# Turning the normed x by transposing DMAs instead of by TensorE, in a new order of steps

## Chip, cores and metric

The kernel runs on one core of a Trainium2 chip. The metric is the device time of one execution in microseconds, as the median of several runs. The profile is of one further execution of the same program.

## What is computed

The inputs are bfloat16. S is 2048 tokens, D is 640 channels, F is 1728.

```python
x  = A_q                                   # (1, 2048, 640)
xn = layernorm(x)                          # (x - mean) / sqrt(var + 1e-5)
# branch A: a long convolution over the tokens, gated by xn
k_shift = causal 4-tap filter of A_k along the tokens, taps A_shift_k per channel
kv = k_shift * A_v
y  = irfft(rfft(kv, padded to 2S) * rfft(A_ssm_k, padded to 2S))[:S] + kv * A_ssm_D
A  = xn * y
# branch B: a gated feed-forward layer
g, u = xn @ B_w_gate, xn @ B_w_up          # (2048, 1728) each
B  = (sigmoid(g) * u) @ B_w_down
out = x + A + B
```

## The kernel before

**Layout.** Token 16p + b lies on partition p in block b, so x and xn are 128 x 16 x 640 tiles. Four blocks of 128 tokens make a group (512 tokens); the feed-forward branch works through groups 0 to 3 as tiles t = 0 to 3. The convolution branch works through five chunks c of 128 channels, each over all tokens.

**Feed-forward branch, per tile.** TensorE needs xn with the channels on the partitions: the tile xnT, 128 x (4 blocks) x (5 channel chunks) x 128, of which there is one buffer for all groups. `xn_mm` transposes a block by five TensorE transposes into a PSUM tile pt, and `xn_ev` copies pt to xnT on ScalarE. For each of 13 slices of 128 columns of F there are a gate product (`gate_mm`, 5 matmuls of 128x128 by 128x512), an up product (`up_mm`), the sigmoid on ScalarE (`gate_ev`) and the product of the two into hT on VectorE (`up_ev`); the last 64 gate and up columns share one product (`both_mm`). Then come 16 halves of down products (`down_mm`, 7 matmuls of 128x320 each), and VectorE adds each finished one to x (`down_ev`). All four blocks of xnT must be there before the first gate product of a tile, and the last reader of xnT in a tile is its `both_mm`. Group 0 is normed and turned ahead of everything, block by block, with small quarter products between; the statistics and norm of groups 1 to 3 are VectorE steps (`ln_norms`, `ln_var`, `ln_xn`) with one small GpSimd step between (`ln_pow`).

**Convolution branch, per chunk.** The transform is a two-stage matrix product. VectorE filters k in two halves of 8 steps (`kv_op`) and turns the filter A_ssm_k (`h_turn`). Stage one (`st1_mm`, 8 matmuls a step, 8 steps a chunk) is evicted (`st1_ev`, 128x1024), written to DRAM (`wr1`) and read back in another layout (`rd2`, tile t). Stage two (`st2_mm`, 16 matmuls of 32x32) is evicted in two halves (`st2_ev`, tile xz), multiplied by VectorE in a shuffle and a product (`prod`), transformed back (`inv1_mm`, 32 matmuls of 32x32), evicted in two halves (`inv1_ev`, tiles ao and kx), written to DRAM (`wr2`) and read back (`rdb`, tiles bi and kx). The last stage (`inv2_mm`, tile psb) is multiplied with xn (`inv2_q`) and added to x (`inv2_x`) on VectorE. Finished parts of x are stored (`store`).

**Queues and order.** Every engine runs its instructions in the order in which the program issues them. After the start (group 0, the first weights, 14.6 us in the profile), that order is written out by hand: each kind of step is a chain under one letter, and a string ORDER says from which chain the next step is taken. Nearly all DMAs are issued by SyncE (SP), in this same order, so a DMA whose wait is not over holds back every DMA behind it. The letters that matter here: g products of the feed-forward branch, s and u their ScalarE and VectorE steps, k the filter of k, l the norm, e and E the turning of a group, a/A, b/B, c/C, d/q the stages of the convolution with their evictions, w, r, W, R its DRAM traffic, m and n the loads, o the stores. A letter F, J, I or Y stands for B, C, A or E with the eviction on VectorE instead of ScalarE; the old string has none of them.

**PSUM.** Two pools: psC (2 buffers of 128x1024 float32) for the stages of the convolution and for pt of group 0; psG (4 buffers of one 512-column bank) for gate, up and down products, psb, and pt of groups 1 to 3.

Of the kernel before, what the change touches and what calls it, by code (L numbers as in the profile page):

```python
# [10 lines left out]
BF16 = mybir.dt.bfloat16  # L11
# [8 lines left out]
P = 128  # L20
NB = S // P
NC = DM // P
# [35 lines left out]
def kernel(  # L58
# [14 lines left out]
    nc = tc.nc  # L73
# [11 lines left out]
    TBd = nc.inline_tensor(tbbits, name="tabTB")  # L85
    SMd = nc.inline_tensor(smbits, name="tabSM")
# [4 lines left out]
    psC = ctx.enter_context(tc.tile_pool(name="psC", bufs=2, space=bass.MemoryType.PSUM))  # L91
    psG = ctx.enter_context(tc.tile_pool(name="psG", bufs=4, space=bass.MemoryType.PSUM))

    ident = res.tile([P, P], BF16, name="ident")
# [4 lines left out]
    TBt = res.tile([P, 2, NB, P], U16, name="TBt")  # L99
    SMt = res.tile([P, 3, 32], U16, name="SMt")  # L100
# [5 lines left out]
    xn = res.tile([P, NB, DM], BF16, name="xn")  # L106
    xnT = res.tile([P, 4, NC, P], BF16, name="xnT")
# [13 lines left out]
    sync = nc.sync  # L121
# [105 lines left out]

    xts = {}

    def xn_mm(g, i):  # L230
        pool, tag = (psG, "g") if g else (psC, "c")
        xts[i] = pt = pool.tile([P, NC, P], BF16, name="pt", tag=tag)
        for c in range(NC):
            nc.tensor.transpose(pt[:, c, :], xn[:, 4 * g + i, c * P:(c + 1) * P], ident[:])  # L234

    def xn_ev(g, i, copy=act_copy):
        copy(out=xnT[:, i, :, :], in_=xts[i][:, :, :])


    sig = {}  # L240
# [246 lines left out]
            nc.tensor.matmul(idle[:, :], lhsT=hT[:, 0, 0:P], rhs=hT[:, 0, :], start=True, stop=True)  # L487

    def turn(i):
        xn_mm(0, i)  # L490
        xn_ev(0, i)


    busy(15)
    for i in range(4):
# [5 lines left out]
        ln_pow(0, i, i + 1)  # L501
    ln_xn(0, 3)
    turn(0)
    busy(2)
    for i in range(4):
        for fc in range(2):
            for u in range(2):
                quarter(u, fc, i)
            if (i, fc) in ((0, 0), (1, 0), (1, 1)):
                turn(1 + i + fc)  # L510
# [2 lines left out]
        up_ev(0, fc)  # L513


    chains = {k: [] for k in "ABCDEHKPRTVWZabcdeghklmnopqrstuw"}

    def step(k, fn, *args):
        chains[k].append((fn, args))
# [16 lines left out]
    def hs(c):  # L536
        return [(load_h, c)]

    def ks(c):
        return [(load_halo, c), (load_k, c, 0, 8), (load_k, c, 8, NB)]  # L540

    def vs(c):
        return [(load_v, c, 0, 8), (load_v, c, 8, NB)]

    for k in ((load_w, sync, 512, 768, 0),
              (load_w, sync, 512, 768, 1),
              (load_taps, 0),
              (sync.dma_start, SMt[:], SMd.ap()),
              (load_w, sync, 768, 1024, 0),
              (load_w, sync, 768, 1024, 1),  # L550
              (load_w, sync, 1024, 1280, 0),
              (load_w, sync, 1024, 1280, 1),
              (load_wd, sync, 0, 7),
              *ks(0),
              (load_w, sync, 1280, FF, 0),
              (load_w, sync, 1280, FF, 1),
              *hs(0),
              *vs(0),
              (load_wd, sync, 7, NFC),
              (sync.dma_start, S1t[:], S1d.ap()),  # L560
              *hs(1),
              (load_x, sync, 1),
              *ks(1),
              *vs(1)):
        step("m", *k)
    for k in ((load_x, sync, 2), (load_x, sync, 3), (sync.dma_start, TBt[:], TBd.ap())):
        step("n", *k)
    step("Z", taps, 0)

# [38 lines left out]
    for g in range(1, 4):  # L608
        for i in range(4):
            step("l", ln_norms, g, i)  # L610
        step("l", ln_var, g, 0, 4)
        step("P", ln_pow, g, 0, 4)
        for i in range(4):
            step("l", ln_xn, g, i)
        for i in range(4):
            step("e", xn_mm, g, i)
            step("E", xn_ev, g, i)

    for b in range(0, 12, 2):
        step("o", store, b, b + 2, 0, 4 * P)  # L620
# [5 lines left out]
    step("o", store, NB - 1, NB, 4 * P, DM)  # L626

    ORDER = """
    mmmmmmmmmmZgmgsmgumgsmgugsgugsmgugskgkugkskgumkgsmkgumkgsmTguHgsHDgumgskkgukgskmgukgskgumkgkmgmutmkm
    auTaAHgAHDagAwlhauaAlglaglguwlgkPkgAulgAllleKeuKwEekaEekaEgkEVVHAgAHDgwughkgkugkskguKrrkaskaAgkAkguw  # L630
    gkskgutkgTskgkKuKaksaAKkgAkaugAwkaksaAkgkwakAgVuAVHasgwHDAauhgAkgkskwbugBrkgBkktbgpBrTkgBpsapsaAuguA
    apKgKswAkaugAkaKkwsakgVHAVgAuDHgswkcugCkgkskCgnuWakaAkgAkgukwbguBrlgBlgulbgBrlgBuglkPpgnulgllleenuEe
    kbEeprgEEgptkBgupBgkaauAgpAkapgswAkaugAkawksaAgkAkguwlcsglCgClbusgrlBWgBkugslpPkaauAgllAlglspwbgBruR
    kgBkscpguCpgCksWbkgBrugBkksbpgBrudBpdgsRqpcqgCqugCqpsWbgBrukgBspbgBrupdBadqsaApRgqAqapgwAqauseeEueaE
    egEEgAgAwaudAdqgwqRqcugCqgCguWbgBrgBugpbpdBrdqgBuqgqpcqgCupgCguWbgBrgBugpspRbgBrugBspcguCpgsCguWbsdr
    BdqgRBqqguqbpsgrBpgBugpspcgCugCsWbguBrdBgqspbqgBupgBspgucpsdCgRqRCqguWbsgBgBugpspgudsdqcqgCqoqdCudqg
    WqqgsqgugoguRRguggugguogodudqogqqogqdoudqogqqogqguogooouo
    """
    left = {k: iter(v) for k, v in chains.items()}
    for k in "".join(ORDER.split()):  # L640
# [33 lines left out]
```

## Time and profile before

| | |
|---|---|
| Runs, median of 3 (lowest to highest) | 239.77 us (239.52 to 239.82) |
| The profiled execution's own time | 240.16 us |
| Its span, first to last instruction | 238.4 us |
| Granted TensorE clock | 1.000 |
| Busy: TensorE (matmul) / VectorE / ScalarE / GpSimd | 232.6 / 190.5 / 140.9 / 11.2 us |
| DMA: bytes, mean rate | 54.82 MB, 230 GB/s |
| DMA: share of the 16 engines, main queue | 81.3% |

The profile gives for each engine its busy time and, in 40 slices of 5.96 us, its busy share in tenths; then the chain of work that ended last, the groups of instructions by line, tile and shape with their mean duration, and the DMAs with their median time from issue to landing. A duration in it is that of one instruction from start to end; matmuls overlap in a pipeline, so what a matmul costs in a row of its kind is read from the chain. A DMA share above 1 in a window means that packets overlap on the engines.

### The profile page before, as it was taken

How to read it: one execution, taken by the hardware profiler on the slowest of the kernel's cores; microseconds unless marked ns; L12 is line 12 of the kernel's file. 1: busy time of each engine (PE TensorE's matmuls, PEld its weight loads, DVE VectorE, ACT ScalarE, POOL GpSimd, SP SyncE). 2: the span in 40 equal slices, each digit the busy share in tenths (PEclk: the TensorE clock that was granted, in tenths of full speed). 3: DMA queues.
4: the chain of work that ended last, by engine and by line, in shares of the span. 5: the costliest groups of instructions: out<-in, count | busy, mean ns of one | idle time of the engine just before them, and what ended most of it. 6: DMA issues, size and time to landing. Idle time of an engine off the chain costs nothing.

```text
span 238.4 us, 5555 instructions
## 1 busy us (share of the span) xinstructions
PE 232.6 (98%) x2265; PEld 134.8 (57%) x2265; DVE 190.5 (80%) x350; ACT 140.9 (59%) x178; POOL 11.2 (5%) x24
## 2 busy tenths in 40 slices
PE   8899999999999999999999999999999999999994
PEld 2664445877555555667754434577664434456772
DVE  4633989999999999999999999865585695968372
ACT  2343322728557898764888787997558858764000
POOL 5210000020000000002000000000000000000000
PEclk9999999999999999999999999999999999999999
DMA  7999999998998999998444889875849795285494
GB/s 213 291 315 236 254 326 294 197 257 236 251 312 252 259 292 292 297 252 313 154 179 143 235 237 265 216 231 202 230 119 223 186 282 126 83 241 145 123 303 137
DMA packets 89119, 54.82 MB, mean 230 GB/s; under 512 B 47814, under 2 KB 83206, under 8 KB 88838
## 3 DMA queue, kind: packets, MB, share of 16 engines
q1 hardware_dynamic: 88150, 53.66, 81.3%
q10 hardware_dynamic: 944, 0.82, 1.1%
q8 instruction: 17, 0.28, 0.5%
q14 instruction: 8, 0.07, 0.1%
HBM read 36.12 MB, written 18.35 MB: 228 GB/s over the span
## 4 chain that ended last, share of the span: by engine, by line
PE 91%; DMA 5%; ACT 2%; issue 0%; ACTq 0%; DVE 0%
PE pd L301 26%; PE pg L257 22%; PE pu L257 22%; PE psb L461 4%; PE ps L360 3%; PE ps L362 3%; PE ps L393 3%; DMA w<-in_B_w_up_dram 3%; PE psa L422 2%; PE pg L278 2%; PE pt L234 2%; DMA d<-t 2%; ACT t L223 1%; PE pu L248 1%; PE pg L248 1%
## 5 line engine op out<-in xcount | busy, mean ns | idle before, releaser
L257 PEld LDWEIGHTS <-w 128*128 128x128 bf16 x500 | 46.4, 98 | 54.4 <-issue 5.3
L301 PE MATMUL pd<-wd,hT 128*128 128x320 bf16 (+2 forms) x448 | 64.3, 299 | 0.0
L257 PE MATMUL pg<-xnT,w 128*128 128x512 bf16 x250 | 62.2, 379 | 0.0
L257 PE MATMUL pu<-xnT,w 128*128 128x512 bf16 x250 | 62.2, 379 | 0.0
L301 PEld LDWEIGHTS <-hT 128*128 128x128 bf16 x448 | 42.3, 98 | 18.5 <-issue 1.7
L266 ACT ACTIVATE sig<-pg 128x512 bf16<-128x512 f32 x52 | 31.3, 605 | 29.8 <-PE pg L257 28.0
L272 DVE TENSOR_TENSOR hT<-sig,pu 128x512 bf16<-128x512 bf16 x52 | 35.2, 680 | 15.5 <-PE pu L257 9.6
L223 ACT CAST t<-ps 128x1024 bf16<-128x1024 f32 x40 | 39.2, 1023 | 12.1 <-DMA d<-t 7.9
L223 ACT CAST xz<-ps 128x1024 bf16<-128x1024 f32 x40 | 38.5, 1017 | 10.6 <-PE ps L393 10.5
L306 DVE TENSOR_TENSOR x<-pd,x 128x320 bf16<-128x320 f32 (+2 forms) x32 | 15.3, 479 | 15.5 <-PE pd L301 15.3
L408 DVE TENSOR_TENSOR xz<-xz 128x2048 bf16<-128x2048 bf16 x20 | 24.3, 1217 | 0.2
L360 PE MATMUL ps<-kvh,S1t 128*128 128x128 bf16 x160 | 21.2, 217 | 0.5 <-ACT t L223 0.5
L362 PE MATMUL ps<-kvh,S1t 128*128 128x128 bf16 x160 | 21.2, 220 | 0.0
L340 DVE TENSOR_TENSOR acc<-acc,tmp 128x1024 bf16<-128x1024 bf16 x30 | 20.7, 689 | 0.6
L338 DVE TENSOR_TENSOR tmp<-kx,sc 128x1024 bf16<-128x1024 bf16 x30 | 20.5, 685 | 0.4
L223 ACT CAST ao<-psa 128x1024 bf16<-128x1024 f32 x16 | 15.6, 1014 | 6.0 <-PE psa L422 3.9
L362 PEld LDWEIGHTS <-S1t 128*128 128x128 bf16 x160 | 15.4, 96 | 2.9 <-issue 0.8
L466 DVE TENSOR_TENSOR yx<-psb,xn 128x512 bf16<-128x512 f32 x20 | 13.8, 690 | 3.9 <-PE psb L461 2.9
L360 PEld LDWEIGHTS <-S1t 128*128 128x128 bf16 x160 | 15.5, 97 | 2.3
L223 ACT COPY xnT<-pt 128x640 bf16<-128x640 bf16 x16 | 10.2, 708 | 10.9 <-PE pt L234 10.6
L198 DVE BATCH_NORM_STATS2 st<-x 128x6 f32<-128x320 bf16 x32 | 13.7, 470 | 2.6 <-DMA x<-in_A_q_dram 2.6
L406 DVE STREAM_SHUFFLE xz<-xz 128x512 f32<-128x512 f32 x20 | 14.5, 725 | 0.0
(44 smaller groups left out, 147.5 us busy)
## 6 DMA issues: line engine op xcount, KB each, us to landing
d<-t SPq DMA_DIRECT2D x20, 512.0 KB, 3.9
t<-d SPq DMA_DIRECT2D x20, 512.0 KB, 5.2
bi<-d SPq DMA_DIRECT2D x8, 512.0 KB, 5.2
d<-ao SPq DMA_DIRECT2D x6, 512.0 KB, 4.1
kx<-in_A_k_dram SPq DMA_DIRECT2D x10, 256.0 KB, 5.1
hn<-in_A_ssm_k_dram SPq DMA_DIRECT2D x20, 128.0 KB, 5.9
kvh<-in_A_v_dram SPq DMA_DIRECT2D x10, 256.0 KB, 5.3
x<-in_A_q_dram SPq DMA_DIRECT2D x3, 640.0 KB
```

Source lines behind the costliest of these rows:

```text
L223: nc.scalar.copy(out=out, in_=in_)
L257: nc.tensor.matmul(pg[:, :], lhsT=w[:, c, u * UP + fc * P:u * UP + (fc + 1) * P], rhs=xnT[:, :, c, :], start=(c == 0), stop=(c == NC - 1))
L266: nc.scalar.activation(sig[fc][:, :], pgs[0, fc][:, :], ACT.Sigmoid)
L272: nc.vector.tensor_tensor(hT[:, fc, :], sig[fc][:, :], pgs[1, fc][:, :], ALU.mult)
L301: nc.tensor.matmul(pd[:, :], lhsT=hT[:, fc, bb * P:(bb + 1) * P], rhs=wd[:, fc, es], start=(fc == 0), stop=(fc == NFC - 1))
L306: nc.vector.tensor_tensor(x[:, 4 * t + bb, es], pds[bb, half][:, :], x[:, 4 * t + bb, es], ALU.add)
L338: nc.vector.tensor_tensor(d["tmp"][:, :, :], kx[:, lo + 3 - m:hi + 3 - m, :], sb(m), ALU.mult)
L340: nc.vector.tensor_tensor(d["acc"][:, :, :], d["acc"][:, :, :], d["tmp"][:, :, :], ALU.add)
L360: nc.tensor.matmul(ps[:, i, 0:P], lhsT=S1[:, b, h, :], rhs=cin[c]["kvh"][:, 0, b, :], start=True, stop=True)
L362: nc.tensor.matmul(ps[:, i, P:2 * P], lhsT=S1[:, b, h, :], rhs=hp[:, b // 2, b % 2, :], start=True, stop=True)
L406: nc.vector.stream_shuffle(z[:, 2, :, :].bitcast(F32), z[:, 1, :, :].bitcast(F32), swap)
L408: nc.vector.tensor_tensor(z[:, 1:3, :, :], z[:, 0:1, :, :].to_broadcast((P, 2, 8, P)), z[:, 1:3, :, :], ALU.mult)
```

## The change

Group 0 is still turned by TensorE. For groups 1 to 3 the five transposes and the copy of each block are replaced by one transposing DMA from SP, `xn_turn`, which reads 128 x 640 of xn and writes 128 x 5 x 128 of xnT. There are 12 of them. The chain E goes, and so do the pt tiles in psG. The order of the first loads is new (x of group 1 stands first), the chain n begins with the table TBt and not with x of group 2, and the whole ORDER string is new. It also moves six evictions to VectorE (F twice, I once, J three times).

```diff
--- before.py
+++ after.py
@@ -227,14 +227,17 @@
 
     xts = {}
 
-    def xn_mm(g, i):
-        pool, tag = (psG, "g") if g else (psC, "c")
-        xts[i] = pt = pool.tile([P, NC, P], BF16, name="pt", tag=tag)
+    def xn_mm(i):
+        xts[i] = pt = psC.tile([P, NC, P], BF16, name="pt", tag="c")
         for c in range(NC):
-            nc.tensor.transpose(pt[:, c, :], xn[:, 4 * g + i, c * P:(c + 1) * P], ident[:])
-
-    def xn_ev(g, i, copy=act_copy):
-        copy(out=xnT[:, i, :, :], in_=xts[i][:, :, :])
+            nc.tensor.transpose(pt[:, c, :], xn[:, i, c * P:(c + 1) * P], ident[:])
+
+    def xn_ev(i):
+        nc.scalar.copy(out=xnT[:, i, :, :], in_=xts[i][:, :, :])
+
+
+    def xn_turn(g, i):
+        sync.dma_start_transpose(xnT[:, i, :, :], xn[:, 4 * g + i, :])
 
 
     sig = {}
@@ -487,8 +490,8 @@
             nc.tensor.matmul(idle[:, :], lhsT=hT[:, 0, 0:P], rhs=hT[:, 0, :], start=True, stop=True)
 
     def turn(i):
-        xn_mm(0, i)
-        xn_ev(0, i)
+        xn_mm(i)
+        xn_ev(i)
 
 
     busy(15)
@@ -513,7 +516,7 @@
         up_ev(0, fc)
 
 
-    chains = {k: [] for k in "ABCDEHKPRTVWZabcdeghklmnopqrstuw"}
+    chains = {k: [] for k in "ABCDHKPRTVWZabcdeghklmnopqrstuw"}
 
     def step(k, fn, *args):
         chains[k].append((fn, args))
@@ -542,28 +545,28 @@
     def vs(c):
         return [(load_v, c, 0, 8), (load_v, c, 8, NB)]
 
-    for k in ((load_w, sync, 512, 768, 0),
+    for k in ((load_x, sync, 1),
+              (load_w, sync, 512, 768, 0),
               (load_w, sync, 512, 768, 1),
-              (load_taps, 0),
-              (sync.dma_start, SMt[:], SMd.ap()),
               (load_w, sync, 768, 1024, 0),
               (load_w, sync, 768, 1024, 1),
+              (load_taps, 0),
+              *vs(0),
               (load_w, sync, 1024, 1280, 0),
               (load_w, sync, 1024, 1280, 1),
-              (load_wd, sync, 0, 7),
-              *ks(0),
               (load_w, sync, 1280, FF, 0),
               (load_w, sync, 1280, FF, 1),
               *hs(0),
-              *vs(0),
+              (load_wd, sync, 0, 7),
               (load_wd, sync, 7, NFC),
+              *ks(0),
+              *ks(1),
+              *hs(1),
               (sync.dma_start, S1t[:], S1d.ap()),
-              *hs(1),
-              (load_x, sync, 1),
-              *ks(1),
+              (sync.dma_start, SMt[:], SMd.ap()),
               *vs(1)):
         step("m", *k)
-    for k in ((load_x, sync, 2), (load_x, sync, 3), (sync.dma_start, TBt[:], TBd.ap())):
+    for k in ((sync.dma_start, TBt[:], TBd.ap()), (load_x, sync, 2), (load_x, sync, 3)):
         step("n", *k)
     step("Z", taps, 0)
 
@@ -613,8 +616,7 @@
         for i in range(4):
             step("l", ln_xn, g, i)
         for i in range(4):
-            step("e", xn_mm, g, i)
-            step("E", xn_ev, g, i)
+            step("e", xn_turn, g, i)
 
     for b in range(0, 12, 2):
         step("o", store, b, b + 2, 0, 4 * P)
@@ -626,15 +628,15 @@
     step("o", store, NB - 1, NB, 4 * P, DM)
 
     ORDER = """
-    mmmmmmmmmmZgmgsmgumgsmgugsgugsmgugskgkugkskgumkgsmkgumkgsmTguHgsHDgumgskkgukgskmgukgskgumkgkmgmutmkm
-    auTaAHgAHDagAwlhauaAlglaglguwlgkPkgAulgAllleKeuKwEekaEekaEgkEVVHAgAHDgwughkgkugkskguKrrkaskaAgkAkguw
-    gkskgutkgTskgkKuKaksaAKkgAkaugAwkaksaAkgkwakAgVuAVHasgwHDAauhgAkgkskwbugBrkgBkktbgpBrTkgBpsapsaAuguA
-    apKgKswAkaugAkaKkwsakgVHAVgAuDHgswkcugCkgkskCgnuWakaAkgAkgukwbguBrlgBlgulbgBrlgBuglkPpgnulgllleenuEe
-    kbEeprgEEgptkBgupBgkaauAgpAkapgswAkaugAkawksaAgkAkguwlcsglCgClbusgrlBWgBkugslpPkaauAgllAlglspwbgBruR
-    kgBkscpguCpgCksWbkgBrugBkksbpgBrudBpdgsRqpcqgCqugCqpsWbgBrukgBspbgBrupdBadqsaApRgqAqapgwAqauseeEueaE
-    egEEgAgAwaudAdqgwqRqcugCqgCguWbgBrgBugpbpdBrdqgBuqgqpcqgCupgCguWbgBrgBugpspRbgBrugBspcguCpgsCguWbsdr
-    BdqgRBqqguqbpsgrBpgBugpspcgCugCsWbguBrdBgqspbqgBupgBspgucpsdCgRqRCqguWbsgBgBugpspgudsdqcqgCqoqdCudqg
-    WqqgsqgugoguRRguggugguogodudqogqqogqdoudqogqqogqguogooouo
+    mmmmmmmmmmgmgsgZuTgmsgumgsgugsgumgsgumgsgllugHsmmguDmHgsmlguglsmgulPgsmmgulglsllgkmugksmmegukgmkeguH
+    geuDgHegukhgkgukgkgknuakaAkgkAgukwgkgunKkgKktKgTukaskaAgkAkaugAwklansaAglwlagVuVAgHsHgADugwshlgulgkP
+    skgulrglsrllgukgskkaauAgkAkgskwgukbskgrBKkgBuKKtapsaTkgApAaugAwkaksaAgkkwaugAVHVAgHDswbugBrkhgBkksbg
+    uBrpgBkepsaaAgueApgkwcpegCuekgCugkWkbugBrkglKBgKlKbugpBrlgBugpgupclgCpgCugWlkPbtugkBTlrglBllsapRaAug
+    pAagkswAkauaAkgkwaskgVAHVdAudDgqRwHcsqgCqkgCqubWskgBkrgBkuapsaAkddpAgqwbugBrqqgBkqsbpgBrupgBskgpcusp
+    gCgCkuWbksgrBFgupbsgkBRpgButcpsgkCpgCuaWskaAgkAkdudwaqRaAkgqAqaekgsqAuawgekAkgwkebugkBekdBduaqrapArg
+    qAqgpwgquckgCJguWkbgkBrkgBukgpRbugpBrgBkgupapaAgAaudAwdqaRaqAqgqwasgAIguwcsgCJduWdqbgBrqqgBqspbguBrp
+    gBspgugpsbugBrFgspcugpCgCsWbguBrgBspbguBRpRgBspgucpsgCgCuWdsdqbgqBqooqdBudoogqpgqsqoogpgqsucugCJgsWg
+    ugguRguRgguggugdudqgqqoddqgqoqgqouqgooogugouo
     """
     left = {k: iter(v) for k, v in chains.items()}
     for k in "".join(ORDER.split()):
```

## The prediction, made before the changed kernel was run

> **What bounds the kernel now.** I read the page first, for the engines' shares along the span; then the chain of waits, the tile that the change takes away, the time by windows, the DMA queue, and last the timeline of the end.
>
> The page, shares of the span and the slices:
>
> ```profile
> PE 232.6 (98%) x2265; PEld 134.8 (57%) x2265; DVE 190.5 (80%) x350; ACT 140.9 (59%) x178; POOL 11.2 (5%) x24
> ...
> PE   8899999999999999999999999999999999999994
> ...
> DVE  4633989999999999999999999865585695968372
> ...
> DMA  7999999998998999998444889875849795285494
> ```
>
> TensorE is never short of work after the start, VectorE is full from the fifth slice to the 26th (about 30 to 155 us), and the DMA engines are full for the first 40 us and nearly so up to 100. Three things are tight at once over the first half; only TensorE is tight to the end. By windows (PE, PEld, DVE, ACT, POOL, clock, DMA share, GB/s):
>
> ```profile
> 30.00:40.00 10.00, 10.00 (x50) 4.73 (x49) 9.03 (x14) 2.90 (x5) 0.42 (x1) 1.00 1.11 312
> 40.00:50.00 10.00, 10.00 (x103) 7.96 (x102) 9.77 (x21) 4.63 (x6) 0.43 (x1) 1.00 0.92 209
> 100.00:110.00 10.00, 10.00 (x110) 6.85 (x108) 9.73 (x26) 5.78 (x6) 1.10 (x1) 1.00 0.88 251
> ```
>
> The granted clock is 1.00, so only the amount of work counts. In the chain (start, length) stand the marks that I count from: the last product of tile 0, the turning of group 1, the first gate product of tile 3:
>
> ```profile
> 38.37 1.08 PE pg L278 x5
> ...
> 53.58 0.84 PE pt L234 x15
> 54.87 0.28 PE pt L234 x5
> ...
> 179.78 1.08 PE pg L257 x5
> ```
>
> **TensorE and ScalarE: what is removed.** The rows of the tile that goes:
>
> ```profile
> L234 PE MATMUL pt<-ident,xn x80: 217/219/230, 7.0 to 159.3; 128*128 128x128 bf16 x80
> L223 ACT COPY xnT<-pt x16: 692/704/747, 7.5 to 160.0; 128x640 bf16<-128x640 bf16 x16
> ```
>
> Of the 80 transposes, 60 go. A row's 219 ns is latency; pipelined, 15 take 0.84 us, or 0.056 each. 60 x 0.056 = **3.36 us**, all on TensorE's path. The 12 copies (12 x 0.704 = 8.4 us of ScalarE) are worth nothing by themselves: ScalarE is busy 59%.
>
> **VectorE: what the new order moves onto it.** Six evictions of 128x1024 go from ScalarE to VectorE (letters F, I, J). VectorE has no such row; ScalarE's takes 1.02 us, two of VectorE's 128x512 reads of PSUM 2 x 0.69 = 1.38. I take 1.3. I then counted each order's steps from both_mm of tile 0 to the first gate of tile 3, priced by the rows (hT 0.68, a convolution step 0.69, x<-pd 0.48, shuffle and product 0.73 + 1.22, turn 1.09, statistics with their aggregate 1.1 a block, and so on) and multiplied by 190.5/204.4 = 0.932: the groups sum to 204.4 us, but neighbours overlap and the page has 190.5. TensorE is priced by the chain (five 128x512 matmuls 1.08, a down half 0.95, a step of the first stage 0.45, of the second 0.36 + 0.11, of the inverse 0.58 + 0.11). Before: TensorE 140.6, VectorE 130.9. After: TensorE 137.8, VectorE 138.5. The slack of 9.7 us is gone: eleven more convolution steps, two of the copies, two products and three inverse steps lie in the stretch, less the norm of group 1, which moved ahead of it. Up to both_mm of tile 2 the old order had VectorE 1.1 over TensorE (118.4 against 117.3) and ran that in 156.44 - 38.37 = 118.1 us, so my pricing is right within 1 us. Cost: 138.5 - 137.8 = **0.7 us** (0 to 3.5: nothing if overlap improves; 138.5/0.98 - 137.8 if VectorE waits 2% of this stretch; it was idle for 2 to 3% of the windows above from 40 us on).
>
> **The transposing DMAs.** Twelve of 128x640, SBUF to SBUF. None is in the trace; from the rows:
>
> ```profile
> q1 hardware_dynamic: 88150, 53.66, 81.3%
> ...
> out_dram<-x SPq DMA_DIRECT2D x3, 160.0 KB, 1.9
> ...
> x<-in_A_q_dram SPq DMA_DIRECT2D x1, 160.0 KB, 3.0
> ```
>
> Lower end: 160 KB at the best rate of any 2 us window (388 GB/s, 34 to 36 us) is 0.42 us. Middle: 88150 packets took 81.3% of 16 x 238.4 us, 35 ns each; if a block moves as 640 runs of 128 elements (40 for each engine), 1.4 us. Upper end: 3.0, if nothing overlaps and each costs what a 160 KB load takes to land. I take 1.0 us of queue time, nearer to the two lower rows because over half of the packets are under 512 B and so cheaper than the mean.
>
> Cover: gate_mm of the next tile needs all four. They wait for both_mm of the tile before. From there to the next gate TensorE has 16.1 us of other work in tile 0 (16 down halves, 15.2, two first-stage steps), 18.9 in tile 1, 23.1 in tile 2. Four at 1.0 plus 2 to land is 6, so tiles 1 and 2 are safe up to 4 us each. While SP waits there, stage-one stores and stage-two loads of chunks 1 to 4 stand behind it, but both_mm is already at the head of TensorE's queue when SP arrives; I price that at nothing, and at some 2 us of a late t<-d if SP came earlier. Tile 0 isn't, since the queue is still full. In the new order 12.6 MB of loads stand ahead; the first seven slices moved 276 GB/s on average, so they are through at 45.7 and landed by about 47.5. The fourth transpose lands at 47.5 + 4 x 1.0 = 51.5; the gate comes at 38.4 + 17.2 = 55.6. Hidden, up to 2 us each.
>
> What stands behind them on SP pays first. Half of v of chunk 1 (needed much later), h of chunk 2, TBt, the first store of stage one, then x of group 2, which the old order loaded some 40 us later: 512 + 1024 + 512 + 640 KB = 2.75 MB, 10 us at 276 GB/s, so x lands at 61.5. VectorE comes to its statistics after 21 convolution steps, 2 turns and 11 evictions, 20.9 us behind 38.4: 59.3. It is 2.2 us late, on an engine without slack, though four buffers of products stand between it and TensorE. I charge a third, **0.7 us** (0 to 2.2). The moved x of group 1 at the head delays the weights by 640 KB, 2.4 us: w up to column 768 is 3.3 MB in, landed by 15, needed at 18.95. Free.
>
> **The end.** After the last inverse product, the old order had 12.67 us of TensorE work until the second inverse:
>
> ```profile
> 215.00 1.93 ACT L223 CAST kx<-psa 128x1024 bf16<-128x1024 f32 x2 [0.93 <-PE psa L422]
> ...
> 216.96 0.36 SPq L438 DMA_DIRECT2D d<-kx  x1
> ...
> 222.29 0.52 SPq L452 DMA_DIRECT2D bi<-d  x1
> ...
> 227.41 1.06 PE L461 MATMUL psb<-bi,TBt 128*128 128x128 bf16 x16
> ```
>
> Evictions 1.93, store 5.3, load 5.0: 12.4, just covered. The new order leaves both_mm and ten down halves, 1.19 + 9.5 = 10.7. One eviction goes to VectorE and the two run side by side, 1.1 to 2.2; store 4.1 to 5.4, load 4.9 to 6.0 by those lines' medians and extremes: 10.2 to 13.7, at mid 11.5. Cost: **0.8 us** (0 to 3).
>
> **Sum.** The profiled execution took 240.16, its span 238.4. 240.16 - 3.36 + 0.7 + 0.7 + 0.8 = 239.0. The median of the runs is 0.39 lower: **238.6 us**. With the three costs between a quarter and one and a half of these, this case alone reaches from 237.0 to 239.7.
>
> **A rule against it.** The Trainium skill, "VectorE: DVE Perf Modes", section "The three transpose paths", puts a 128x128 bf16 transpose at 390 ns on TensorE and 1309 ns by DMA, and advises TensorE where PSUM will do. This trace disagrees on the first figure: 219 ns latency, 56 in a pipeline. On the second no run here shows it. "Advanced Engine Details and Errata", section "X-Bar Transpose (TRN2)", says on the contrary that such DMAs go at 350 to 400 GB/s, an estimate of 0.45 us a block, with which x would land in time and the sum be 237.9.
>
> **The rivals.**
> Full gain: VectorE, x and the end hide, as the old order's 1.1 us of excess cost only 0.8; 236.4. For it: TensorE idles almost nowhere now. Against: three places without slack. 0.20.
> VectorE becomes the bound: 2% of waits in its stretch, 3.5 instead of 0.7, and with the end and x 241.4; with those hidden 239.9. For it: 138.5 against 137.8. 0.13, about half within 0.2%.
> Slower, by the queue in the first 75 us: the new order puts TBt and x of groups 2 and 3 (2.4 MB) there, and a transpose that holds the rings for 2 to 3 us delays all behind it. Each microsecond above 1.0 costs 4, since VectorE waits for x at 59 and TensorE then for stage two. It decides from 1.3 us a block on (238.6 + 4 x 0.3 is the old time); at 2.0 the time is 242.6, at 3.0 246.6. For it: DMA share above 1 there. Against: TensorE has 4 us of cover at the gate. 0.28.
> The five squares of a block go one after another, each at the 1.9 us of the quickest 160 KB row: 9.5 a block, 38 a group, against covers that end at 55.6 - 47.5 = 8, 18.9, 23.1: 30 + 19 + 15 later, about 302 us. No row speaks for it. 0.03. (By the skill's 1309 ns: 6.5 a block, 26 a group, 18 + 7 + 3 later, about 266.)
>
> **How the numbers follow.** The forecast has 0.36, of it 0.32 faster by over 0.2% (below 239.29; 0.2% is about what a measurement here can tell) and 0.04 within. With the full gain: faster 0.52. Within: 0.04 + 0.06 = 0.10. Slower: 0.07 + 0.28 + 0.03 = 0.38. The range 235.9 to 245.0 takes in the full gain and the slow queue up to 2.6 us a block; it leaves out some 0.12 above and 0.03 below.
>
> **What would show it.** Right: 20 rows of pt instead of 80; TensorE busy near 229; a transposing DMA landing in 2 to 7 us with the first gate of tile 1 near 55.6 and no wait for xnT; small waits of VectorE for x near 60 and of psb at the end. Wrong: TensorE waiting for xnT or t<-d between 55 and 85 us, VectorE idle for x by more than 3 us, or SP's queue held for over 2 us by one transpose.

## The result, and the profile after

| | before | after |
|---|---|---|
| Median of the runs (lowest to highest) | 239.80 us (239.52 to 240.39) | 248.80 us (247.25 to 250.43) |
| The profiled execution's own time / span | 240.16 / 238.4 us | 247.25 / 245.5 us |
| Busy: TensorE / VectorE / ScalarE | 232.6 / 190.5 / 140.9 us | 230.8 / 196.3 / 127.7 us |
| DMA main queue: packets, MB, share | 88150, 53.66, 81.3% | 96214, 55.62, 86.2% |

The ratio after to before is **1.0373, with a 95% interval of 1.0298 to 1.0448**: 9.0 us slower where 1.2 us faster was forecast, and outside the range. (In all ratios of this document runs over 1.5% above the quickest of the same kernel are left out, so a ratio can stand lower than the median of all runs.)

The page of the changed kernel, the same rows as before:

```profile
PE 230.8 (94%) x2204; PEld 131.9 (54%) x2205; DVE 196.3 (80%) x356; ACT 127.7 (52%) x160; POOL 11.1 (5%) x24
...
PE   8799999989689999998998999999997999999995
...
DVE  4633688799589998999999999899995796778264
...
DMA  7999998987998899999999876699978764885544
...
q1 hardware_dynamic: 96214, 55.62, 86.2%
...
PE 50%; DVE 21%; DMA 17%; issue 5%; ACT 3%; SPq 2%; ACTq 0%; DVEq 0%
```

TensorE, which was never short of work, now stands idle in the eleventh slice (about 61 to 67 us), and VectorE too. In the chain of waits DMAs hold 17%. The DMA queue moved 96214 - 88150 = 8064 more packets, 672 for each transposing DMA: the prediction's middle row, 640 runs of 128 elements, with a few more.

The tile that the change takes away, pt, and the DMAs that stand in for it (duration on the issuing queue as least, median and greatest, in ns; then from issue to landing, in us):

```profile
L233 PE MATMUL pt<-ident,xn x20: 219/219/220, 6.6 to 12.7; 128*128 128x128 bf16 x20
```

```profile
L240 SPq DMA_TRANSPOSE xnT<-xn x12: 1212/1410/2647, 44.2 to 168.5; - x12
...
DMA to landing us min/median/max: 2.7/4.3/6.5
```

Landing is as forecast. The first line is what the prediction had no term for: each transposing DMA occupies SP itself for 1.2 to 2.65 us, where a plain DMA takes SP 0.48 us at the median. (Plain ones are held up too at times: 29 of the 159 take over 1 us.) SP's timeline around the first four turnings (start, length, line, what, how many):

```profile
44.16 1.31 SPq L240 DMA_TRANSPOSE xnT<-xn  x1
45.52 1.48 SPq L169 DMA_DIRECT2D kvh<-in_A_v_dram  x1
47.10 4.95 SPq L240 DMA_TRANSPOSE xnT<-xn  x3
...
52.64 2.72 SPq L139 DMA_DIRECT2D hn<-in_A_ssm_k_dram  x4
55.40 0.43 SPq L644 DMA_DIRECT2D TBt<-tabTB  x1
55.94 0.38 SPq L377 DMA_DIRECT2D d<-t  x1
56.35 0.43 SPq L129 DMA_DIRECT2D x<-in_A_q_dram  x1
```

The four turnings end at 52.05, and the first store of stage one (`d<-t`) and x of group 2 go out at 55.94 and 56.35. Who waits for them, from the timelines of TensorE, ScalarE and VectorE (in brackets the idle time before and its releaser):

```profile
57.20 1.24 PE L260 MATMUL pg<-xnT,w 128*128 128x512 bf16 x5
...
63.73 1.01 ACT L223 CAST t<-ps 128x1024 bf16<-128x1024 f32 x1 [2.78 <-DMA d<-t]
...
64.80 0.22 PE L363 MATMUL ps<-kvh,S1t 128*128 128x128 bf16 x1 [2.39 <-ACT t L223]
65.22 0.89 DVE L198 BATCH_NORM_STATS2 st<-x 128x6 f32<-128x320 bf16 x2 [2.84 <-DMA x<-in_A_q_dram]
```

The first gate product of tile 1 has no wait: the turned block itself is in time. The eviction of stage one waits for the buffer t, which the late store has not yet emptied; TensorE's stage one waits for that eviction; and VectorE waits 2.84 us for x. At the end of the kernel there is no wait: after the last inverse product TensorE runs its down halves without a gap until the second inverse.

```profile
224.49 1.01 ACT L223 CAST kx<-psa 128x1024 bf16<-128x1024 f32 x1 [1.12 <-PE psa L425]
...
225.41 9.67 PE L304 MATMUL pd<-wd,hT 128*128 128x320 bf16 x70
234.92 1.06 PE L464 MATMUL psb<-bi,TBt 128*128 128x128 bf16 x16
```

### The profile page after: what moved, and what is told of

Its sections match the earlier page's. It is cut to its first block, busy times and chain, and to the rows that moved or that the text cites. A ratio compares the mean times of both kernels' runs of the same rounds, so it can differ in the third digit from the quotient of the medians.

```text
span 245.5 us, 5452 instructions
## 1 busy us (share of the span) xinstructions
PE 230.8 (94%) x2204; PEld 131.9 (54%) x2205; DVE 196.3 (80%) x356; ACT 127.7 (52%) x160; POOL 11.1 (5%) x24
## 3 DMA queue, kind: packets, MB, share of 16 engines
q1 hardware_dynamic: 96214, 55.62, 86.2%
HBM read 36.12 MB, written 18.35 MB: 222 GB/s over the span
## 4 chain that ended last, share of the span: by engine, by line
PE 50%; DVE 21%; DMA 17%; issue 5%; ACT 3%; SPq 2%; ACTq 0%; DVEq 0%
PE pg L260 16%; PE pu L260 15%; DMA d<-t 7%; PE pd L304 7%; DMA w<-in_B_w_up_dram 3%; DVE hT L275 3%; PE psb L464 3%; DMA d<-ao 3%; DVE tmp L341 2%; DVE x L309 2%; PE ps L396 2%; ACT t L223 2%; PE psa L425 2%; DVE xz L411 2%; DVE xz L409 2%
## 5 line engine op out<-in xcount | busy, mean ns | idle before, releaser
L223 ACT CAST t<-ps 128x1024 bf16<-128x1024 f32 x39 | 38.0, 1019 | 30.0 <-PE ps L365 17.5
L223 ACT CAST xz<-ps 128x1024 bf16<-128x1024 f32 x38 | 36.7, 1016 | 12.6 <-PE ps L396 11.1
L363 PE MATMUL ps<-kvh,S1t 128*128 128x128 bf16 x160 | 20.9, 218 | 3.7 <-ACT t L223 2.4
L365 PE MATMUL ps<-kvh,S1t 128*128 128x128 bf16 x160 | 21.0, 220 | 0.0
L223 ACT CAST ao<-psa 128x1024 bf16<-128x1024 f32 x14 | 13.6, 1020 | 6.8 <-PE psa L425 6.7
L323 DVE STREAM_TRANSPOSE kvh<-hn 128x512 f32<-128x512 f32 x10 | 10.7, 1089 | 2.1 <-DMA hn<-in_A_ssm_k_dram 2.1
```

The costliest lines, as they stand in the source:

```text
L223: nc.scalar.copy(out=out, in_=in_)
L363: nc.tensor.matmul(ps[:, i, 0:P], lhsT=S1[:, b, h, :], rhs=cin[c]["kvh"][:, 0, b, :], start=True, stop=True)
L365: nc.tensor.matmul(ps[:, i, P:2 * P], lhsT=S1[:, b, h, :], rhs=hp[:, b // 2, b % 2, :], start=True, stop=True)
```

## The experiments

Two theories. **SP's hold**: the loss is the time for which a transposing DMA occupies SP, so that the loads and stores behind it go out late. **The order**: the new ORDER string loses time by itself (VectorE without slack, or some wait it makes), whatever turns x. A rival to the first is that the many small packets of a turning are slow on the DMA engines, or hold up others there. That the turned x comes late is out by the 57.20 row above.

**e1: the new order, groups 1 to 3 not turned at all.**

```diff
-            step("e", xn_turn, g, i)
+            step("e", lambda: None)
```

> The new order with the twelve transposing DMAs left out, so groups 1 to 3 use group 0's transposed x (that part of the computation is missing). Theory Q (the transposes hold SP and the rings in the first 110 us; the order itself is sound): 236.5 to 239, the 3.4 us of TensorE are seen at last. Theory O (the new order of loads and steps loses the time by itself: x of group 1 at the head, TBt and x of groups 2 and 3 early): 245 or more, with the waits for d<-t near 64 us and for h near 45 us still there. Something between the two divides the loss.

**e2: the new order, groups 1 to 3 turned by TensorE** (the body of `xn_turn` is five transposes into a psG tile and a ScalarE copy).

> The new order, but each transposing DMA replaced by five TensorE transposes and the copy on ScalarE at the same place. Theory Q: e1 plus 3.4 us, 240 to 242. Theory O: e1 plus 3.4 where TensorE is the bound, less where it waits anyway: 247 to 249.

**e3: the new order, each turning a plain DMA of the same 160 KB.**

```diff
-        sync.dma_start_transpose(xnT[:, i, :, :], xn[:, 4 * g + i, :])
+        sync.dma_start(xnT[:, i, :, :], xn[:, 4 * g + i, :].rearrange("p (c e) -> p c e", c=NC))
```

> The new order with each transposing DMA replaced by a plain DMA of the same 160 KB from xn to xnT (no turning, so the products use the wrong layout). If transposing is what costs (1.2 to 2.6 us of SP for each, in place of some 0.4): within 1.5 us of e1, SP's issue 0.3 to 0.6 us each. If any DMA at that place of SP's queue costs the same, because it waits for both_mm and holds the loads behind it: as the changed kernel, 247 to 250.

**e4: the old order, only group 3 turned by DMA**, at the places of its `xn_mm` steps.

```diff
     def xn_mm(g, i):
+        if g == 3:
+            sync.dma_start_transpose(xnT[:, i, :, :], xn[:, 4 * g + i, :])
+            return
...
     def xn_ev(g, i, copy=act_copy):
+        if g == 3:
+            return
```

> The old order, with only group 3 (where the DMA share is 0.7 and the turning stands right behind both_mm, 20 us before the next gate product) turned by four transposing DMAs at the place of the TensorE transposes. Theory Q and theory O alike: hidden, 1.1 us less on TensorE, 238.4 to 239.3. If a transposing DMA costs more than 2 us of rings even there (stage-one stores and stage-two loads behind it late): 240 to 242.

Measured:

| | median us | ratio to before (95%) |
|---|---|---|
| e1, no turning | 242.11 | 1.0112 (1.0061 to 1.0164) |
| e2, TensorE | 245.48 | 1.0241 (1.0186 to 1.0296) |
| e3, plain copies | 243.37 | 1.0159 (1.0109 to 1.0209) |
| e4, old order, group 3 | **238.66** | **0.9959 (0.9936 to 0.9982)** |

Both theories hold a part. The kernel before took 239.61 in these runs; without the 60 transposes the old order's work would be 239.61 - 3.36 = 236.25. The new order with nothing to turn takes 242.11: **the order alone loses 5.9 us**. Plain copies add 1.3, and that they transpose adds another 248.80 - 243.37 = 5.4: **the DMAs cost 6.7 us together**. TensorE's own turning costs 245.48 - 242.11 = 3.37 in the same order, so in this order the DMAs are dearer than what they replace. At the median the copies hold SP for 0.4 of the time, at about the same landing:

```profile
L240 SPq DMA_DIRECT2D xnT<-xn x12: 464/542/4022, 42.9 to 162.6; - x12
...
DMA to landing us min/median/max: 3.1/4.7/6.8
```

The median hides one copy of 4.0 us, which stands in group 1 (e3's SP):

```profile
42.88 0.68 SPq L240 DMA_DIRECT2D xnT<-xn  x1
...
44.45 5.32 SPq L240 DMA_DIRECT2D xnT<-xn  x3
```

Over all twelve the copies hold SP for 10.8 us and the turnings for 20.3; in group 1 alone for 5.8 and 6.05.

Where the time goes is seen when the traces are cut at TensorE's marks (first full gate product of tile 0, then the last products `both_mm` of a tile and the first gate of the next, in turn), us:

| | to both 0 | to gate 1 | to both 1 | to gate 2 | to both 2 | to gate 3 | to both 3 | to end |
|---|---|---|---|---|---|---|---|---|
| before | 23.74 | 21.03 | 37.58 | 20.65 | 38.81 | 23.34 | 37.21 | 21.57 |
| after | 23.74 | 18.35 | 40.70 | 20.76 | 41.74 | 26.89 | 37.03 | 21.18 |
| e1 | 23.73 | 17.20 | 37.48 | 20.78 | 41.47 | 25.69 | 37.39 | 21.22 |
| e3 | 23.74 | 18.39 | 38.40 | 20.77 | 41.66 | 25.31 | 37.45 | 21.11 |
| e4 | 23.74 | 21.04 | 36.93 | 20.65 | 38.91 | 22.31 | 37.21 | 21.54 |

Between after and e1 the stages differ by 5.4 us (these are the profiled executions, of 247.25 and 241.73 us): 3.2 in tile 1, where the waits shown above lie, 1.2 ahead of it, 1.2 ahead of tile 3 and 0.3 in tile 2, less 0.4 in tile 3. Orders place their work differently, so rows of the old and the new order compare only as sums. SP in e1 over the same stretch:

```profile
46.74 1.93 SPq L139 DMA_DIRECT2D hn<-in_A_ssm_k_dram  x4
48.72 0.43 SPq L644 DMA_DIRECT2D TBt<-tabTB  x1
52.92 0.35 SPq L377 DMA_DIRECT2D d<-t  x1
53.31 0.43 SPq L129 DMA_DIRECT2D x<-in_A_q_dram  x1
```

Here SP has nothing to do from 49.2 to 52.9; it waits for the data of the first store. Before that it waits from 43.5 to 45.9. That slack of 3.8 and 2.4 us is what four turnings have to fit into. The first store by kernel (its data evicted; issued by SP; landed, from the chain, in e1 from its slowest store of 5.4 us; then the eviction that needs the buffer, and TensorE's wait for that):

| | data ready | issued | landed | eviction starts | TensorE waits |
|---|---|---|---|---|---|
| e1 | 52.89 | 52.92 | by 58.3 | 59.7, no wait | 0 |
| e3 | 53.42 | 53.45 | 60.5 | 60.60 | 0 |
| after | 54.12 | 55.94 | 63.6 | 63.73 | 2.39 |
| e12 (below) | 53.93 | 56.55 | 64.4 | 64.48 | 3.32 |

The copies use up the slack and no more: their store goes out as soon as its data is there. In after it waits 1.8 us for SP, in e12 2.6. Against e1, the store of after lands at least 5.3 us later: 1.2 by later data, 1.8 by SP, and 2.3 or more by a longer landing (7.7 us against 5.4 at most), of which the copies show most (7.1).

What makes SP later in after than in e3 is only in small part the turnings' own hold. From the first gate product of tile 0, which comes 0.7 us later in after, SP is through with TBt 2.5 us later. The four turnings make up 0.3 of that. Two plain loads among and behind them make up 1.7 (half of v 1.48 us against 0.74, the last load of h 1.38 against 0.43), and 0.5 lies ahead of the first turning. Why these loads were held isn't shown; the packets of the turnings stay a rival.

**e5: the transposing DMAs issued by ScalarE instead of SP** (`nc.scalar.dma_start_transpose`).

> The changed kernel with the twelve transposing DMAs issued by ScalarE's queue instead of SP's. If the price of a transpose is the time that it holds SP (1.2 to 2.6 us each, with loads and stage-one stores behind it): near the plain copies, 243 to 245, and the rings no longer half empty between 52 and 58 us. If it is the rings' own time (the transposing packets are slow or block the others): 247 to 250 as before. If ScalarE's evictions behind a waiting transpose are late instead: above 250.

Inconclusive: median 248.95, but the four runs lie between 243.62 and 253.61, so no ratio is given. In the one that was profiled the hold is the same on ScalarE's queue, and the turnings, which no longer stand behind SP's loads, went out at 39.2 to 44.7, ahead of rows of h. VectorE then waited 5.08 us for h, and TensorE's stage one for VectorE:

```profile
L240 ACTq DMA_TRANSPOSE xnT<-xn x12: 1215/1280/2282, 39.2 to 169.3; - x12
```

```profile
48.34 1.09 DVE L323 STREAM_TRANSPOSE kvh<-hn 128x512 f32<-128x512 f32 x1 [5.08 <-DMA hn<-in_A_ssm_k_dram]
...
54.29 0.27 PE L363 MATMUL ps<-kvh,S1t 128*128 128x128 bf16 x1 [3.32 <-DVE kvh L346]
```

The stage to gate 1 took 24.81, part of it at a granted clock of 0.50 (53.2 to 60.0 us); the stage of tile 1, with SP free, took 36.66. That agrees with SP's hold as the cause in tile 1, without proving it.

**e6: the new order, group 1 turned by TensorE, groups 2 and 3 by DMA.**

> The changed kernel with group 1 turned by TensorE and groups 2 and 3 by the transposing DMAs. If the loss sits in the first 75 us, where the rings are full: 244 to 245.5 (the order with TensorE turning everything, 245.5, less up to 2.2 us of TensorE). If each transpose costs the same wherever it stands: 247 to 248.

244.47 us, ratio 1.0169 (1.0120 to 1.0218): as expected. The median falls by 4.3 though TensorE works 1.1 us more, so by the medians most of what the turnings cost goes with the four of group 1. The profiled run fits: its tile 1 takes 39.49 us, with some 1.7 us lost to a slow clock (last section), and the 37.8 left are near e1's 37.48.

**e7: e1 with one filter tap of k left out**, 20 VectorE steps; VectorE's busy time falls from 196.5 to 185.9 us.

```diff
-            step("k", kv_op, c, n)
+            if n % 8 in (1, 2):
+                step("k", lambda: None)
+            else:
+                step("k", kv_op, c, n)
```

> The new order without any turning of groups 1 to 3 (as the first experiment, 242.1) and with one of the four filter taps left out: 20 VectorE steps of 0.69 us fewer (both parts of the computation are missing). If VectorE is what binds the new order from the first gate product of tile 1 to that of tile 3: 237 to 239, with these stages at TensorE's own 36, 20, 41 and 24 us. If the order's loss is DMA waits: 241 to 242.5.

241.12 us, ratio 1.0070 (1.0041 to 1.0098): 1.0 us less than e1, not 3 to 5. **VectorE as the bound of the new order falls.**

**e8: x of group 2 loaded ahead of TBt** (the first two entries of chain n swapped), all else as in after.

> The changed kernel with one exchange in the chain of late loads: x of group 2 ahead of the table TBt (both stay where the chain's letter stands). If VectorE's 2.8 us wait for x near 65 us is a cause: 246 to 247.5, the wait gone. If it only shadows the late stage-one store (TensorE waits for it in any case): 248 to 250.

246.91 us, ratio 1.0215 (1.0162 to 1.0267). VectorE's wait for x near 65 us is gone, TensorE's wait for the eviction is not:

```profile
63.75 0.22 PE L363 MATMUL ps<-kvh,S1t 128*128 128x128 bf16 x1 [1.98 <-ACT t L223]
```

So x late costs some 2 us by the medians (3.8 by the ratios), and the late store remains. The profiled tile 1 takes 40.49 us, against 40.70 in after, but some 1.7 of it are lost to a slow clock (last section); without them it is 1.9 shorter. The four runs scatter too much to split it closer.

**e9: the old order, groups 1 to 3 all turned by DMA** (e4's edit with `if g:` in place of `if g == 3:`).

> The old order with groups 1 to 3 turned by the transposing DMAs, each at the place where TensorE turned that block. In groups 1 and 2 only four down halves and some 0.5 to 1 us of stage one lie between the last transpose and the next gate product, 4.5 to 5 us, against four transposes that hold SP for 1.3 us and land 4 us after issue (some 8 us). Theory Q: TensorE waits some 3 to 4 us for xnT in each of tiles 1 and 2, less 3.4 of work: 242 to 245, the wait named at the gate product. Were the price of a transpose only its own bytes: 237 to 239.

250.04 us, ratio 1.0433 (1.0409 to 1.0456). The mechanism was named and the size missed by 5 us or more. In the old order the turnings of groups 1 and 2 stand too near to the gate that needs them:

```profile
62.72 2.29 PE L262 MATMUL pg<-xnT,w 128*128 128x512 bf16 x5 [4.56 <-DMA xnT<-xn]
...
125.19 2.29 PE L262 MATMUL pg<-xnT,w 128*128 128x512 bf16 x5 [4.23 <-DMA xnT<-xn]
```

The two waits are 8.8 us; less 3.36, that gives 5.4 over before. Most of the other 5.0 is seen in the 2.29 us that five matmuls took, elsewhere 1.24: the clock had fallen (last section).

**e10: e1 with x of group 1 loaded after the first weights** and not at the head.

> The new order without turning (first experiment, 242.1), with x of group 1 moved from the head of the loads to behind w up to column 1024. If x at the head delays the first up weights (TensorE waited 1.45 us for them instead of 0.25): 241.3 to 241.8, first full gate product near 14.4 us. If the start only varies from run to run: 241.8 to 242.5.

242.00 us, ratio 1.0100 (1.0075 to 1.0126): the same as e1. x of group 1 at the head of the loads costs nothing. Its stage to gate 1 is 18.33 with no turning at all, so the 1.2 us by which after exceeds e1 there can't be laid to the turnings with certainty.

**e11: the new order mended by what had been learnt**: group 1 on TensorE, x of group 1 later, x of groups 2 and 3 ahead of TBt.

> The new order with group 1 turned by TensorE, x of group 1 behind w up to column 1024, and the late loads in the order x of group 2, x of group 3, TBt; groups 2 and 3 by transposing DMAs. The named DMA causes in the first 75 us are then all taken away: 242.5 to 244 (from 244.5), still slower than before, since some 5 us of the new order's loss show without any turning.

A miss: 247.42 us (243.99 to 248.15), ratio 1.0242 (1.0165 to 1.0318). In the profiled run tile 1 is short (37.02), but tile 2 took 45.51: the order of the loads moved a wait there, and a slow clock followed it.

```profile
126.42 1.86 PE L470 MATMUL psb<-bi,TBt 128*128 128x128 bf16 x16 [2.92 <-DMA bi<-d]
```

**e12: e3 with SP held longer.** After each plain copy come three writes of 256 bytes that nobody reads.

```diff
+        for j in range(3):
+            sync.dma_start(scratch[12 * g + 3 * i + j:12 * g + 3 * i + j + 1, :], ident[0:1, :])
```

> The third experiment (plain copies of 160 KB in place of the transposes, 243.4) with three 256-byte writes to DRAM behind each copy: hardly any bytes, but some 1 us more of SP's time for each, so that a copy holds SP about as long as a transpose. If the hold of SP is what makes a transpose dearer than a copy: 246.5 to 250, with the rings half empty near 52 to 58 us. If it is the rings' time for transposing packets: 243 to 245.

251.55 us, ratio 1.0441 (1.0367 to 1.0515): above the expected range. In group 1 a block now occupies SP for 0.47 to 0.69 us by its copy and 1.03 to 1.47 by the three writes, about what a transposing DMA takes, and nothing is transposed. The loss is there in full, and with it TensorE's wait, 3.32 us. (ScalarE's waits for `d<-t` come to 14.7 us, against 9.0 in after; but e3 has 9.6, so their sum doesn't measure the loss.) The windows from 46 to 52 and 52 to 58 us show what the DMA engines do while SP is late: after, e1 and e12 in turn (columns: window, its length, TensorE, weight loads, VectorE, ScalarE, GpSimd busy, clock, DMA share, GB/s).

```profile
46.00:52.00 6.00, 5.01 (x43) 3.60 (x42) 5.90 (x10) 0.00 (x0) 0.42 (x1) 1.00 1.15 206
52.00:58.00 6.00, 6.00 (x50) 4.26 (x48) 5.86 (x11) 2.59 (x3) 0.00 (x0) 1.00 0.63 150
```

```profile
46.00:52.00 6.00, 6.00 (x55) 4.59 (x54) 5.86 (x11) 1.04 (x2) 0.00 (x0) 1.00 1.09 233
52.00:58.00 6.00, 6.00 (x53) 4.27 (x51) 5.90 (x11) 2.24 (x4) 0.00 (x0) 1.00 0.97 330
```

```profile
46.00:52.00 6.00, 4.54 (x41) 3.31 (x40) 5.90 (x11) 0.00 (x0) 0.42 (x1) 1.00 0.78 210
52.00:58.00 6.00, 6.00 (x48) 4.09 (x46) 5.86 (x12) 2.58 (x3) 0.00 (x0) 1.00 0.48 132
```

With h of chunk 2, TBt, the first store and x of group 2 (2.75 MB) still to go out at 52 us, the DMA engines run at 150 GB/s in after and 132 in e12, against 330 in e1 and 258 in e3. They are not full; they have been given nothing, because SP is behind. Engines too full would show the opposite.

But the hold of copies and writes is not all that e12 brings. SP stood still from 45.7 to 48.35, and its waits name the landing of a table (waited for, us in all, times, longest):

```profile
SPq L241 <- DMA S1t<-tabS: 2.6, 1, 2.6
```

SP has no such wait ahead of its turnings in after or its copies in e3. Without it e12's first store would have gone out near 53.95, when its data was ready. So e12 shows that SP being late costs this much without any transposing; it doesn't show that a hold as long as a turning's is enough to make SP late. Behind TensorE's wait of 3.32 us the clock was slow too, some 1.7 us lost (last section); with the 2.6 that is about e12's surplus over after in the profiled runs, 4.3 us, though nothing shows that the two simply add.

**The version that beats both kernels is e4.** It keeps the old order and gives only group 3 to the DMA: 238.66 us, 0.95 below before and 10 below the change. The profile is as clean as before's:

```profile
PE 231.5 (98%) x2245; PEld 133.9 (57%) x2245; DVE 190.4 (80%) x350; ACT 138.8 (59%) x174; POOL 11.2 (5%) x24
...
PE 97%; ACT 1%; DVE 0%; issue 0%
```

```profile
L232 SPq DMA_TRANSPOSE xnT<-xn x4: 1259/1276/1484, 156.7 to 160.9; - x4
...
DMA to landing us min/median/max: 3.1/3.9/4.7
```

At 157 to 161 us SP has room, and some 21 us of other work lie ahead of the gate: 0.95 of the 1.12 us is gained.

## Why the prediction was wrong, point by point

**TensorE, -3.36: right.** In e4 the stage to gate 3 shrinks from 23.34 to 22.31, 1.03 for 1.12. e2 less e1 is 3.37 by the medians; that it comes so near is luck, since their intervals leave some 1.8 us either way.

**The transposing DMAs, 1.0 us of queue time each: the step that failed.** It priced the transfer (pieces, landing, cover of the gate), and that part held: landings of 2.7 to 6.5 us, and the gate at 57.20 without a wait. It had no term for the time in which issuing a turning occupies SP, though SP's rows stood in the trace beside. Its sentence on SP, that what stands behind the waiting turnings is priced "at nothing", treated the queue as a place to wait and not as an engine with work of its own. Measured: 1.41 us a turning at the median, 20.3 us of SP over the twelve, against 0.54 and 10.8 for copies; no transposing DMA in any of the traces held its queue for less than 1.2. The loss is 6.7 us, 1.3 for the copies and 5.4 more for their transposing (e1, e3). That SP being late costs such a loss is shown by the first store and by e12. That the turnings' own hold is what makes it late is not. Of the 4.2 us between the profiled runs of e3 and after, 2.3 lie in tile 1, where the holds of group 1 are nearly equal (5.8 and 6.05 us); the turnings of group 2 hold SP 5.1 us longer than copies, and tile 2 is 0.1 us longer. The turnings also move in 640 pieces or more a block, plain loads among them are held longer, and the first store lands more slowly. How a turning makes SP late stays open. The Trainium skill, "DMA: Bandwidth & Descriptors", section "Issuing engines are not separate DMA queues", says that the time a sequencer takes to initiate a DMA is usually small beside the DMA itself. These traces differ for a transposing one: 1.41 of 4.3 us to landing.

**x of group 2, +0.7: right place, too small.** It was to land at 61.5 and to be needed at 59.3; it was there at 65.2 and needed at 62.4. VectorE's wait of 2.84 exceeds the bound of 2.2, and e8 puts its price at some 2 us, not a third of the wait. The twin of this wait, the first store, which stood directly ahead of x on the same queue, had no term at all, and its 2.39 us fell on TensorE.

**VectorE, +0.7: about right as a size, wrong as the account of the order.** Its price for an eviction held (1.3, measured 1.22), and 10.6 us less work on VectorE bring 1.0 us (e7). But the order alone loses 5.9 us where the terms of VectorE, x and the end came to 2.2: a second failed step, a price for the order that was too small. In e1's trace TensorE stands idle for 3.7 us between the first `both_mm` and the last, in seven pieces of 0.2 to 1.0 (stage two waiting for an eviction of t, the inverse for a product xz), against 0.5 before; and it is busy 1.5 us longer there than before less the 3.36. That is 4.7 of the 5.9; the start varies besides, from 14.05 to 15.11 us between profiled runs and 16.85 in e7's. Adding up the work of each engine over 140 us can't see these: by the waits, one step and its eviction or product stand too close. Which exchange of letters makes them wasn't tried, so the cause of the order's loss stays open.

**The end, +0.8: wrong.** The stage is 21.18, shorter than before's 21.57. **x of group 1 at the head, free: right** (e10).

**The rivals.** The case "slower, by the queue in the first 75 us" named the place, the late x and TensorE after it, and had the sign; its price hung on how long a block holds the rings, and at the measured 1.41 us it would have given 238.6 + 4 x 0.41 = 240.2. The range ended at 245.0, since no case added a loss of the order to a loss of the queue; the two together are what happened. Four turnings held SP for over 2 us, which it had named as a sign of being wrong. (A slip on which nothing hangs: the fifth slice begins at 23.8 us, not at 30.)

## What to carry to other kernels

Price a DMA three times: by its bytes, by its landing, and by the time for which it occupies the queue that issues it; look for who stands behind it there, for that is who pays. A queue that feeds the whole core has slack only where its timeline shows a gap (here 3.8 us ahead of the first store, and room at 157 us), and of the exchanges tried here only the one at 157 us paid. When a change brings a new order of steps, run that order with the exchanged operation taken out: here that alone showed 5.9 of the 9 us.

## What the runs showed of the hardware

Behind waits of TensorE the granted clock can fall to 0.50 and stay there for several microseconds of full work. The windows of e9 (columns as above):

```profile
121.00:122.00 1.00, 0.00 (x0) 0.00 (x0) 1.00 (x3) 1.00 (x2) 0.00 (x0) 1.00 1.07 377
...
124.00:125.00 1.00, 0.00 (x0) 0.10 (x1) 1.00 (x2) 0.00 (x0) 0.00 (x0) 0.50 1.23 264
...
126.00:127.00 1.00, 1.00 (x4) 0.44 (x3) 0.00 (x0) 0.00 (x0) 0.00 (x0) 0.50 1.18 396
...
129.00:130.00 1.00, 1.00 (x4) 0.43 (x3) 0.00 (x0) 0.42 (x1) 0.00 (x0) 0.50 0.00 0
130.00:131.00 1.00, 1.00 (x12) 0.62 (x10) 0.46 (x1) 0.08 (x1) 0.00 (x0) 0.87 0.00 0
```

TensorE is idle from 121.0 to 125.2 and runs at half speed until 130.3. Half of these last 5.1 us is lost, so the wait of 4.23 us costs 2.5 more; the other wait of e9 (4.56) costs 1.35 more (0.50 until 65.4), and the two together 3.9 of the 5.0 us left open above. In e11 a wait of 2.92 us was enough, with the clock at 0.50 until 129.7: 1.65 more; in e12 one of 3.32. Shorter ones sufficed too: 1.98 us in e8, and two of 1.08 and 0.53 close together in e6. Here are the windows on the two sides of the fall, of e8 and then of e6:

```profile
60.92:64.33 3.41, 1.43 (x19) 1.14 (x18) 3.34 (x10) 1.64 (x3) 0.00 (x0) 1.00 1.04 368
64.33:67.75 3.42, 3.42 (x16) 1.76 (x14) 1.54 (x4) 0.77 (x1) 0.00 (x0) 0.50 1.25 262
```

```profile
88.95:92.37 3.42, 1.81 (x22) 0.64 (x21) 1.17 (x2) 2.96 (x4) 0.18 (x1) 1.00 0.76 192
92.37:95.79 3.42, 3.42 (x24) 1.01 (x22) 2.29 (x5) 1.90 (x3) 0.00 (x0) 0.50 1.02 301
```

Yet in the profiled run of after, waits of 2.39 and 1.73 us left it at 1.00, and so did one of 2.08 in e12. The length of the wait alone doesn't decide. The stretches at 0.50 in the middle of the runs lasted 3.4 us, or twice that. The Trainium skill, "TensorE: Matmul & The Clock Gate", section "Part 1: The HAM clock gate", tells of the same two states, half speed after an idle window of about 3.4 us and full speed after as long a stretch of work, in windows that run freely. The 0.50 agrees, and so does 3.4 us as the length of a slow stretch; that 2.0 us of idle time in the 3.4 us before the fall sufficed (e8), and 1.6 in e6, is less than it states. Such a wait of the bound engine isn't priced by its length alone: those of e9 and e11 cost 30 to 60% more. It doesn't explain the spread of the runs of the changed kernel, of which the slowest has a mean clock of 1.000.
